# A transformer MLP on one Trainium2 core: the first loads, the transposes of the first x block and its shifted copies rearranged

## The chip, the cores and the metric

The kernel runs on one core of one Trainium2 chip. The metric is device time in microseconds (us) of one execution, as a median of several runs. Beside it stands one profiled execution, whose trace gives the start and the duration of every instruction on TensorE (PE, with its weight loads as PEld), VectorE (DVE), ScalarE (ACT), GpSimd (POOL) and SyncE (SP), and the DMA transfers.

## What is computed

The reference, with B = 1, S = 2048, D = 576, F = 4608, all inputs bfloat16:

```python
h = jnp.einsum("bsd,df->bsf", x, w1) + b1
r = jnp.where(h > zero, h, zero)
h = r * r
out = jnp.einsum("bsf,fd->bsd", h, w2) + b2
```

So two matrix products with a squared ReLU between them. D = 576 is four chunks of 128 and a tail of 64.

## The kernel before, in words

**Blocks.** The 2048 rows of x are cut into four blocks of 512 rows. For each block the first product makes h transposed (F on partitions, 36 tiles of 128), ScalarE adds b1 and applies ReLU (line 176), VectorE squares (line 177). The second product is made in two parts: `phase_t` gives the last 128 output columns transposed, `phase_b` the first 448 columns. The order is blocks 0 and 1 through the first product, then both through the second, then blocks 2 and 3 likewise.

**The first product has two forms.** `a_full` makes 4 of the 36 tiles with four matmuls of 128 rows (chunks k = 0 to 3 of D, weights in `w1n`) and, for the 64-row tail, a `pair` of two matmuls that use the lower and the upper half of the array at the same time (weights in `w1n8`, lines 203 and 205). `a_rows` makes the other 32 tiles wholly in such pairs of 64-row matmuls (lines 188 and 190), 9 pairs for two tiles, with weights in `w1_h`. Its lower and upper halves need every 64-row chunk of x transposed in both partition halves. So the transposed block `xTw` has nine windows of 512 columns, and the shifted windows are made by copies from one partition half to the other (`dup_windows`, lines 119 and 120).

**How x gets transposed.** Blocks 1 to 3 come by transposing DMAs. Block 0 comes as four plain row tiles `x_sb` (j = 0 to 3, 128 rows each) and is transposed on TensorE (`x_transpose`, line 149) into PSUM tiles `tb`, from which `x_copies` (lines 156 to 159) moves them to `xTw`: chunks 0 and 2 and the last 128 columns on VectorE, chunks 1 and 3 on ScalarE. There are five transposes for each row tile: four chunks, and the last 128 columns once more, whose upper half is the 64-column tail.

**The start, in TensorE's order.** Seven matmuls on constants (`WARM`, line 63) fill the time until x is there. Then: ten transposes of row tiles 0 and 1; `part(0, 0)`, which is four matmuls of chunk 0 over the first 256 columns (line 227); five transposes of tile 2; `part(0, 1)` and `part(0, 2)`; five transposes of tile 3; `part(0, 3)`, `part(1, 0)`; one transpose that makes the bias columns `b1T` (lines 166 and 167); `part(1, 1)` to `part(1, 3)`; two pairs; then `a_rows(0)`. All of this order is written out by hand, each engine's instructions stay in program order.

**The loads.** SP's DMA queue has, in order: x tile 0, `w1n` chunks 0 and 1, x tile 3, `w1n` chunks 2 and 3, then `w1_h` in pieces with the two halves of `w1n8` (32 KB each) after the first pair, later x block 1, b2, w2 in four pieces. ACT's queue has x tiles 1 and 2. GpSimd's queue has b1 and a column of b2. Eight DMA semaphores are used in turn on the SP and ACT queues, so an issue waits until the eighth DMA before it has landed.

**PSUM** has eight banks in two pools of four, `ps_h` and `ps_o`. In the first `a_full`, two accumulators lie in each pool, and the transposes use banks of both.

Of the kernel before, what the change touches and what calls it, by code (L numbers as in the profile page):

```python
# [11 lines left out]
BF16 = mybir.dt.bfloat16  # L12
# [5 lines left out]
def kernel(  # L18
# [40 lines left out]
    wps = ps_o.tile([P, 512], FP32, name="wps", tag="po")  # L59
    ones = nc.const_aps.tensor(1.0, [P, 512], BF16)  # L60
    WARM = [512] * 6 + [128]
# [5 lines left out]
    w1n8 = wpool.tile([P, G // 2, P], BF16, name="w1n8")  # L67
# [6 lines left out]
    def load_w1n(eng, k):  # L74
        keep(eng.dma_start(out=w1n[:, k, :], in_=w1[k * P:(k + 1) * P, 0:GW]))

    def load_w1n8(eng, h):
        src = w1[NK * P:D, 0:GW].rearrange("p (i h f) -> p i h f", h=2, f=P)
        keep(eng.dma_start(out=w1n8[h * H:(h + 1) * H, :, :], in_=src[:, :, h, :]))
# [4 lines left out]

    load_x(nc.sync, 0)
    load_x(nc.scalar, 1)
    load_w1n(nc.sync, 0)
    load_x(nc.scalar, 2)
    load_w1n(nc.sync, 1)
    load_x(nc.sync, 3)  # L90
    for k in range(2, NK):
        load_w1n(nc.sync, k)
# [3 lines left out]
    b1_rows = const.tile([P, P], BF16, name="b1_rows")  # L96
    nc.gpsimd.memset(b1_rows[:], 0.0)
    nc.gpsimd.dma_start(out=b1_rows[0:NFT, :], in_=b1.rearrange("(ft p) -> ft p", p=P))
    b2_col = const.tile([P, 1], BF16, name="b2_col")
    nc.gpsimd.dma_start(out=b2_col[:], in_=b2[DM:D].rearrange("(d o) -> d o", o=1))  # L100
    b2T = const.tile([P, 1], FP32, name="b2T")
    nc.gpsimd.tensor_copy(out=b2T[:], in_=b2_col[:])
    warm = const.tile([P, 1], FP32, name="warm")
    keep(nc.scalar.activation(out=warm[:], in_=nc.const_aps.tensor(0.0, [P, 1], FP32), func=ACT.Relu))

# [25 lines left out]
    W2CH = 9  # L131
# [9 lines left out]
    tb_po = [ps_o.tile([P, 2, HS], BF16, name="tb", tag="po") for _ in range(2)]  # L141
    tb_ph = [ps_h.tile([P, 2, HS], BF16, name="tb", tag="ph") for _ in range(4)]
    half_banks = [tb_ph, None]

    def x_transpose(j, k):
        h, q = divmod(j, 2)
        qc = slice(q * P, (q + 1) * P)
        bank, slot, c0 = (half_banks[h][k], 0, k * P) if k < NK else (half_banks[h][2], 1, D - P)
        keep(nc.tensor.transpose(bank[:, slot, qc], xs[:, j, c0:c0 + P], ident[:]))  # L149

    def x_copies(h):
        hc = slice(h * HS, (h + 1) * HS)
        for k in range(NK):
            src = half_banks[h][k][:, 0, :]
            if k % 2 == 0:
                keep(nc.vector.tensor_copy(out=xT0[:, O + k, hc], in_=src))  # L156
            else:
                keep(nc.scalar.copy(out=xT0[:, O + k, hc], in_=src))  # L158
        keep(nc.vector.tensor_copy(out=xT0[:, E3, hc], in_=half_banks[h][2][:, 1, :]))  # L159


    b1T = const.tile([P, NFT], FP32, name="b1T")

    def make_b1T():
        b1T_ps = ps_o.tile([P, P], BF16, name="b1T_ps", tag="po")
        keep(nc.tensor.transpose(b1T_ps[:], b1_rows[:], ident[:]))  # L166
        keep(nc.vector.tensor_copy(out=b1T[:], in_=b1T_ps[:, 0:NFT]))
# [27 lines left out]
    def a_full(sb, order):  # L195
        xT = xT_blk[sb]
        banks = []
        for g in range(G):
            pool, tag = (ps_o, "po") if g < 2 else (ps_h, "ph")
            banks.append(pool.tile([P, SB], FP32, name="pn", tag=tag))  # L200

        def pair(i, start, stop):
            keep(nc.tensor.matmul(banks[2 * i][:], lhsT=w1n8[0:H, i, :], rhs=xT[0:H, SPC, :],  # L203
                             start=start, stop=stop, skip_group_check=order == "k_outer"))
            keep(nc.tensor.matmul(banks[2 * i + 1][:], lhsT=w1n8[H:P, i, :], rhs=xT[H:P, E3, :],  # L205
# [13 lines left out]
        else:  # L219
            if order == "k_outer":  # L220
                tb_new = [ps_h.tile([P, 2, HS], BF16, name="tb", tag="ph") for _ in range(2)]
                half_banks[1] = tb_new + tb_po

# [7 lines left out]
                for j in range(2):  # L231
                    for k in range(NK):
                        x_transpose(j, k)
# [126 lines left out]
```

## Time and profile before

| | |
|---|---|
| median of 4 runs | 291.17 us (290.93 to 291.5) |
| the profiled execution | 291.13 us |
| its span, from the first to the last instruction | 289.4 us |
| first matmul of line 188 (`a_rows(0)` begins) | 10.04 us after the span's start |
| TensorE busy | 285.2 us (99%) |
| VectorE busy | 78.5 us (27%) |
| ScalarE busy | 96.7 us (33%) |

The time of the profiled execution is 1.7 us more than its span. The page gives busy times by engine; the chain of waits follows the last instruction back through what released each step; the timeline gives start and duration of merged groups of instructions, where "x10" means ten instructions and the duration reaches from the first start to the last end. Matmuls overlap: the last one's own duration is part of a group's duration, and the rate is read from starts. All times are counted from the span's start.

### The profile page before, as it was taken

What the parts mean: (1) busy time and instruction counts of PE and PEld (TensorE: products, weight loads), DVE (VectorE), ACT (ScalarE), POOL (GpSimd) and SP (SyncE); (2) the same over time, 40 slices, a digit from 0 to 9 for tenths busy, and PEclk for the clock granted to TensorE, in tenths of its full rate; (3) what the DMA queues carried; (4) which work ended last, traced back from release to release, by engine and by line L of the source; (5) the groups of instructions that cost most, each with busy time, mean ns of one, the idle gap of its engine ahead of it and who ended that gap; (6) DMA issues with size and microseconds to landing.
All of it is one profiled execution on the core that took longest, in us unless ns stands there. A gap on an engine that the chain in (4) does not pass through costs nothing.

```text
span 289.4 us, 4693 instructions
## 1 busy us (share of the span) xinstructions
PE 285.2 (99%) x2027; PEld 139.3 (48%) x2032; DVE 78.5 (27%) x176; ACT 96.7 (33%) x154; POOL 2.3 (1%) x10
## 2 busy tenths in 40 slices
PE   8999999999999999999999999999999999999996
PEld 4544444444444555555544444444444455555555
DVE  1644554444500200000025444444440001100001
ACT  2666666666500000000027667666670000000000
POOL 3000000000000000000000000000000000000000
DMA  6999999400001100000000000000000110000000
GB/s 195 214 242 187 315 388 226 87 0 2 0 18 26 47 16 18 16 16 18 16 16 2 1 2 0 2 0 2 0 2 0 36 39 16 16 16 20 32 16 18
DMA packets 31605, 16.52 MB, mean 57 GB/s; under 512 B 15700, under 2 KB 31584, under 8 KB 31584
## 3 DMA queue, kind: packets, MB, share of 16 engines
q1 hardware_dynamic: 31232, 15.91, 22.1%
q8 instruction: 16, 0.26, 0.4%
q10 hardware_dynamic: 288, 0.30, 0.4%
q14 instruction: 5, 0.04, 0.1%
q0 software_dynamic: 64, 0.01, 0.0%
HBM read 11.36 MB, written 2.36 MB: 47 GB/s over the span
## 4 chain that ended last, share of the span: by engine, by line
PE 97%; DMA 1%; DVE 0%; issue 0%
PE ph L188 42%; PE po L289 38%; PE pt L270 11%; PE pn L209 4%; PE pn L227 1%; DMA x_sb<-in_x_dram 1%; PE tb L149 1%; PE ph L190 1%; PE pn L203 1%; DVE o_sb L291 0%; DVE xTw L156 0%; DVE xTw L159 0%; PE b1T_ps L166 0%; PE pn L205 0%
## 5 line engine op out<-in xcount | busy, mean ns | idle before, releaser
L188 PE MATMUL ph<-xTw,w_h 64*128 64x512 bf16 x576 | 124.6, 376 | 0.0
L190 PE MATMUL ph<-xTw,w_h 64*128 64x512 bf16 x576 | 124.6, 376 | 0.0
L289 PE MATMUL po<-w_sb,hT 128*128 128x448 bf16 (+2 forms) x612 | 109.4, 341 | 0.0
L176 ACT ACTIVATE r<-ph,b1T 128x512 bf16<-128x512 f32 x128 | 81.1, 685 | 41.6 <-PE ph L190 41.6
L188 PEld LDWEIGHTS <-w_h 64*128 64x128 bf16 x576 | 54.1, 94 | 68.3
L289 PEld LDWEIGHTS <-hT 128*128 128x128 bf16 x612 | 58.5, 98 | 51.0
L177 DVE TENSOR_TENSOR hT<-r 128x512 bf16<-128x512 bf16 x144 | 61.2, 426 | 75.9 <-ACT r L176 75.5
L190 PEld LDWEIGHTS <-w_h 64*128 64x128 bf16 x576 | 54.1, 94 | 0.0
L291 DVE TENSOR_TENSOR o_sb<-po,b_bc 128x448 bf16<-128x448 f32 (+2 forms) x17 | 10.2, 597 | 125.8 <-PE po L289 125.8
L270 PE MATMUL pt<-hT,w_sb 128*128 128x512 bf16 x142 | 31.3, 379 | 0.1
L176 ACT ACTIVATE r<-pn,b1T 128x512 bf16<-128x512 f32 x16 | 10.3, 688 | 61.0 <-PE pn L205 59.6
L270 PEld LDWEIGHTS <-w_sb 128*128 128x128 bf16 x144 | 14.1, 98 | 17.0
L273 ACT ACTIVATE oT<-pt,b2T 128x512 bf16<-128x512 f32 x4 | 2.8, 688 | 28.3 <-PE pt L270 28.3
L209 PE MATMUL pn<-xTw,w1n 128*128 128x512 bf16 x45 | 10.4, 379 | 0.4 <-issue 0.3
L209 PEld LDWEIGHTS <-w1n 128*128 128x128 bf16 x48 | 4.5, 98 | 6.0 <-issue 0.8
L227 PE MATMUL pn<-xTw,w1n 128*128 128x256 bf16 x32 | 4.2, 273 | 0.0
L63 PE MATMUL wps<-const-bfloat16-1.0 128*128 128x512 bf16 (+1 forms) x7 | 2.8, 581 | 0.8 <-PEq L344 0.8
L227 PEld LDWEIGHTS <-w1n 128*128 128x128 bf16 x32 | 2.9, 99 | 0.7 <-DMA w1n<-in_w_dram 0.5
L156 DVE COPY xTw<-tb 128x256 bf16<-128x256 bf16 x4 | 1.1, 292 | 6.5 <-PE tb L149 6.5
L119 DVE COPY xTw<-xTw 64x2048 bf16<-64x2048 bf16 x4 | 2.8, 689 | 0.2
L120 DVE COPY xTw<-xTw 64x2048 bf16<-64x2048 bf16 x4 | 2.8, 688 | 0.1
L158 ACT COPY xTw<-tb 128x256 bf16<-128x256 bf16 x4 | 1.3, 375 | 3.5 <-PE tb L149 3.5
(23 smaller groups left out, 15.9 us busy)
## 6 DMA issues: line engine op xcount, KB each, us to landing
w_sb<-in_w_dram SPq DMA_DIRECT2D x4, 1296.0 KB, 11.7
w_h<-in_w_dram SPq DMA_DIRECT2D x14, 288.0 KB, 6.5
out_dram<-o_sb SPq DMA_DIRECT2D x15, 112.0 KB, 1.7
w_h<-in_w_dram SPq DMA_DIRECT2D x4, 144.0 KB, 3.7
w1n<-in_w_dram SPq DMA_DIRECT2D x4, 128.0 KB, 3.9
out_dram<-ot SPq DMA_DIRECT2D x4, 128.0 KB, 2.0
x_sb<-in_x_dram ACTq DMA_DIRECT2D x2, 144.0 KB, 2.9
x_sb<-in_x_dram SPq DMA_DIRECT2D x2, 144.0 KB, 3.4
```

What stands on the lines that cost most here:

```text
L63: keep(nc.tensor.matmul(wps[:, 0:n], lhsT=ones[:, 0:P], rhs=ones[:, 0:n], start=True, stop=True))
L149: keep(nc.tensor.transpose(bank[:, slot, qc], xs[:, j, c0:c0 + P], ident[:]))
L176: keep(nc.scalar.activation(out=r[:], in_=bank[:], func=ACT.Relu, bias=b1T[:, ft:ft + 1], scale=1.0))
L177: keep(nc.vector.tensor_tensor(out=hTs[sb][:, ft, :], in0=r[:], in1=r[:], op=ALU.mult))
L188: keep(nc.tensor.matmul(bx[:], lhsT=w1_h[0:H, LO_C[i], jc], rhs=xT[0:H, LO_W[i], :], start=(i == 0), stop=(i == NC - 1)))
L190: keep(nc.tensor.matmul(by[:], lhsT=w1_h[H:P, UP_C[i], jc], rhs=xT[H:P, UP_W[i], :], start=(i == 0), stop=(i == NC - 1)))
L203: keep(nc.tensor.matmul(banks[2 * i][:], lhsT=w1n8[0:H, i, :], rhs=xT[0:H, SPC, :], start=start, stop=stop, skip_group_check=order == "k_o ...
L209: keep(nc.tensor.matmul(banks[g][:], lhsT=w1n[:, k, g * P:(g + 1) * P], rhs=xT[:, O + k, :], start=start, stop=stop))
L227: keep(nc.tensor.matmul(banks[g][:, hc], lhsT=w1n[:, k, g * P:(g + 1) * P], rhs=xT[:, O + k, hc], start=(h == 0 and k == 0), stop=False, s ...
L270: keep(nc.tensor.matmul(pt[:], lhsT=w2_sb[:, ft, DM:D], rhs=hT[:, ft, :], start=(i == 0), stop=(i == NFT - 1)))
L289: keep(nc.tensor.matmul(po[:, 0:d1 - d0], lhsT=hT[:, ft, jj * P:(jj + 1) * P], rhs=w2_sb[:, ft, d0:d1], start=(i == 0), stop=(i == NFT - 1)))
L291: keep(nc.vector.tensor_tensor(out=o_sb[:, d0:d1], in0=po[:, 0:d1 - d0], in1=b2_bc[:, d0:d1], op=ALU.add))
```

## The change

- **Loads.** ACT's queue has `w1n` chunk 0 first, then x tiles 2 and 3 and `w1n` chunk 3, and after ScalarE's table load b1. SP's queue has x tiles 0 and 1, `w1n` chunks 1 and 2, both halves of `w1n8` (now all 512 columns in each half, 64 KB each), then `w1_h`. GpSimd issues no DMA; the column of b2 goes to SP behind `w1_h`. w2 comes in two pieces in place of four.
- **Transposes.** Four for each row tile, 16 in all. The 64 tail columns of two row tiles are put side by side by GpSimd (`xs8`), and one transpose does both tiles: two transposes in all (`transpose_tails`, into `tl`).
- **Copies out of PSUM.** VectorE takes six of the eight chunk copies, ScalarE the last two. Four copies of 64 partitions move the tails from `tl` to the two windows where the pairs read them.
- **Shifted copies of block 0.** ScalarE makes the lower windows E to E+2 (64 x 1536, `dup_windows_first`); VectorE the upper ones (64 x 2048) and one lower window (64 x 512).
- **Order and banks.** Row tiles 2 and 3 are transposed after `part(0, 0)` and `part(0, 1)`; the bias transpose comes after `part(1, 1)`. All four accumulators of the first `a_full` lie in `ps_o`. The last warm-up matmul has 256 columns in place of 128.

The diff, cut to its core:

```diff
-    WARM = [512] * 6 + [128]
+    WARM = [512] * 6 + [256]
...
-    w1n8 = wpool.tile([P, G // 2, P], BF16, name="w1n8")
+    w1n8 = wpool.tile([P, GW], BF16, name="w1n8")
...
     load_x(nc.sync, 0)
-    load_x(nc.scalar, 1)
-    load_w1n(nc.sync, 0)
+    load_w1n(nc.scalar, 0, 1)
+    load_x(nc.sync, 1)
     load_x(nc.scalar, 2)
-    load_w1n(nc.sync, 1)
-    load_x(nc.sync, 3)
-    for k in range(2, NK):
-        load_w1n(nc.sync, k)
+    load_w1n(nc.sync, 1, 2)
+    load_x(nc.scalar, 3)
+    load_w1n(nc.sync, 2, 3)
+    load_w1n(nc.scalar, 3, 4)
...
-    nc.gpsimd.dma_start(out=b1_rows[0:NFT, :], in_=b1.rearrange("(ft p) -> ft p", p=P))
+    keep(nc.scalar.dma_start(out=b1_rows[0:NFT, :], in_=b1.rearrange("(ft p) -> ft p", p=P)))
+    for h in range(2):
+        load_w1n8(nc.sync, h)
+    xs8 = const.tile([P, RT, H], BF16, name="xs8")
+    for h in range(2):
+        keep(nc.gpsimd.tensor_copy(out=xs8[:, 2 * h:2 * h + 2, :], in_=xs[:, 2 * h:2 * h + 2, NK * P:D]))
...
-    W2CH = 9
+    W2CH = 18
...
+    tb = [[ps_h.tile([P, 4, HS], BF16, name="tb", tag="ph") for _ in range(2)] for _ in range(2)]
+    def x_transpose(j):
         h, q = divmod(j, 2)
+        hc = slice(h * HS, (h + 1) * HS)
+        for bank in range(2):
+            for k in range(2 * bank, 2 * bank + 2):
+                keep(nc.tensor.transpose(tb[h][bank][:, k % 2, q * P:(q + 1) * P], xs[:, j, k * P:(k + 1) * P], ident[:]))
+            for k in range(2 * bank, 2 * bank + 2) if q == 1 else ():
+                copy = nc.scalar.copy if h == 1 and bank == 1 else nc.vector.tensor_copy
+                keep(copy(out=xT0[:, O + k, hc], in_=tb[h][bank][:, k % 2, :]))
...
+    def dup_windows_first():
+        keep(nc.scalar.copy(out=xT0[0:H, E:E + 3, :], in_=xT0[H:P, O:O + 3, :]))
+    def transpose_tails():
+        tl = ps_h.tile([P, 2, P], BF16, name="tl", tag="ph")
+        for h in range(2):
+            keep(nc.tensor.transpose(tl[:, h, :], xs8[:, 2 * h:2 * h + 2, :], ident[:]))
+        x8 = xT0.rearrange("p c (h q t) -> p c h q t", h=2, q=2)
+        for q in range(2):
+            keep(nc.vector.tensor_copy(out=x8[H:P, E3, :, q, :], in_=tl[q * H:(q + 1) * H, 0:2, :]))
+        for q in range(2):
+            keep(nc.vector.tensor_copy(out=x8[0:H, SPC, :, q, :], in_=tl[q * H:(q + 1) * H, 0:2, :]))
+        keep(nc.vector.tensor_copy(out=xT0[H:P, SPC:SPC + 4, :], in_=xT0[0:H, O:O + 4, :]))
+        keep(nc.vector.tensor_copy(out=xT0[0:H, E3, :], in_=xT0[H:P, O + 3, :]))
...
                 for j in range(2):
-                    for k in range(NK):
-                        x_transpose(j, k)
-                for j in range(2):
-                    x_transpose(j, NK)
-                x_copies(0)
-                part(0, 0)
-                for k in range(NK + 1):
-                    x_transpose(2, k)
-                part(0, 1)
+                    x_transpose(j)
+                for k in range(2):
+                    part(0, k)
+                    x_transpose(2 + k)
+                dup_windows_first()
                 part(0, 2)
-                for k in range(NK + 1):
-                    x_transpose(3, k)
-                x_copies(1)
-                dup_windows(0)
+                transpose_tails()
                 part(0, 3)
-                part(1, 0)
-                make_b1T()
-                for k in range(1, NK):
+                for k in range(NK):
                     part(1, k)
+                    if k == 1:
+                        make_b1T()
```

## The prediction

> **What bounds the kernel now.** I read four views in this order: the head of the page, the waits of TensorE behind the start, the chain of waits over the first 11 us, and the timeline of TensorE over the same stretch.
>
> The first part of the page says that TensorE is the bound:
>
> ```profile
> span 289.4 us, 4693 instructions
> PE 285.2 (99%) x2027; PEld 139.3 (48%) x2032; DVE 78.5 (27%) x176; ACT 96.7 (33%) x154; POOL 2.3 (1%) x10
> ```
>
> The waits of TensorE between 10 us and the end hold one line, 0.3 us of issue and no wait for another engine or a DMA. So from the first matmul of line 188, at 10.04 us, to the end the stream is dense, and 289.4 - 10.04 = 279.4 us follow whatever the start looks like. The change touches nothing in TensorE's list behind that point. The question is when `a_rows(0)` begins, and whether its weights come in time. The chain of waits over the start:
>
> ```profile
> 0.74 2.92 DMA x_sb<-in_x_dram
> ...
> 3.70 1.26 PE tb L149 x10
> ...
> 4.98 0.29 DVE xTw L156
> 5.28 0.21 DVE xTw L159
> ...
> 5.53 0.40 PE tb L149 x4
> ...
> 5.96 1.19 PE pn L227 x8
> 7.15 0.28 PE tb L149 x5
> 7.43 0.87 PE pn L227 x8
> ```
>
> The reader is to see that the chain is the landing of x tile 0 (3.65 us), then TensorE, broken once by VectorE's copies at 5 us, then TensorE. The timeline of TensorE gives the rates:
>
> ```profile
> 0.78 2.83 PE L63 MATMUL wps<-const-bfloat16-1.0 128*128 128x512 bf16 x7 [0.78 <-PEq L344]
> 3.70 1.25 PE L149 MATMUL tb<-ident,x_sb 128*128 128x128 bf16 x10
> 4.80 0.60 PE L227 MATMUL pn<-xTw,w1n 128*128 128x256 bf16 x4
> 5.26 0.67 PE L149 MATMUL tb<-ident,x_sb 128*128 128x128 bf16 x5
> 6.99 0.44 PE L149 MATMUL tb<-ident,x_sb 128*128 128x128 bf16 x5
> 8.19 1.47 PE L227 MATMUL pn<-xTw,w1n 128*128 128x256 bf16 x12
> ```
>
> To be seen here: twelve matmuls of 256 columns in 1.47 us, the last of them 0.27 long, give (1.47 - 0.27) / 11 = 0.109 us each. Five transposes in 0.44 us, the last 0.22, give 0.056. But the first ten transposes take 1.25, the last 0.31, so about 0.107: until 4.64 TensorE runs at half rate, and at 4.80 at full rate, although the windows view prints a granted clock of 1.00 throughout. Call this the flip, at about 4.7 us. A pair of 64-row matmuls takes 0.215 (124.6 us / 576 on the page's line of L188).
>
> Check of the old start with these rates: 20 + 1 transposes x 0.056 = 1.18; 32 matmuls x 0.109 = 3.49; two pairs 0.43; about ten transposes at half rate, 0.5 more; together 5.60. From 3.70 to 10.04 are 6.34, so about 0.74 us are gaps. The starts in the trace give them: 0.06 before 4.80, 0.22 before 5.53 (the copy of line 159 frees a PSUM bank), 0.20 before 5.96 and 0.13 before 6.54 (`w1n` chunks 1 and 2 landing), 0.10 before the first pair at 9.60 (nothing waited for; 128-row to 64-row matmuls).
>
> **The change, part by part.**
>
> *Landing times.* By the issues view with windows round single issues, before: x tile 1 (ACT, first) 0.74 + 2.73 = 3.47; tile 0 (SP, first) 3.65; tile 2 (ACT, second) 1.16 + 3.06 = 4.21; chunk 0 (SP, second) 1.20 + 3.18 = 4.38; chunk 1 1.69 + 4.22 = 5.91; tile 3 6.12; chunk 2 6.49; chunk 3 7.07. After, by place in its queue: chunk 0 (ACT, first) about 3.4, tile 0 (SP, first) 3.65, tile 2 (ACT, second) 4.2, tile 1 (SP, second) as the old chunk 0 and 16 KB longer, 4.43. So tile 1 comes 1 us later, and it is now the second thing that TensorE asks for.
>
> *The new start, added up.* Tile 0's four transposes at half rate from 3.70: 0.43, until 4.13. Then TensorE waits for tile 1: 4.43 plus the 0.05 that tile 0 took from landing to its first transpose, 4.48. **This wait of 0.35 is new**; everything on TensorE is queued behind it. VectorE's first copy waits for the second transpose of tile 1 (4.48 + 0.11 = 4.59). In the old rows a transpose at 4.10 released a copy at 4.45 that ended at 4.75 and released the matmul at 4.80: 0.70. With the flip on the way I take 0.65: `part(0, 0)` starts at 5.24, against 4.80. The other transposes of tile 1 are inside that, so **0.44 is lost here**. From there: 32 matmuls x 0.109 = 3.49; 8 + 2 + 1 transposes x 0.056 = 0.62; the 0.10 ahead of the pairs; two pairs 0.43; together 4.64. Before, 10.04 - 4.80 = 5.24 went into the same stretch, as it held as many matmuls and transposes and the three gaps of 0.55 (and 0.05 of odd starts). **0.60 is gained here**, provided that nothing new waits. `a_rows(0)` begins at 5.24 + 4.64 = 9.88, 0.16 earlier.
>
> *Do the waits stay away?* Needed against there, by the same sum: chunk 1 at 5.24 + 0.44 + 0.22 = 5.90; tile 3 at 6.34; chunk 2 at 6.56; chunk 3 at 7.11. Before, the same bytes had landed at 5.91, 6.12, 6.49 and 7.07, but tile 3 stood behind chunk 1. The trace bounds the new times from both sides. While both queues were loaded (2.50 to 3.25) the DMA rate was 363 GB/s: the 272 KB of chunk 1 and tile 3 take 0.75, landing about 5.1. With one queue (4.00 to 4.75) it was 229 GB/s: about 1.2, landing at 5.6, or 6.1 with the last engine as late as for the old tile 3; then chunk 1 costs 0.2, and chunk 2 (landing up to 7.07) up to 0.3 more. I take nothing, as the queue that runs dry in the old rows after 4 us stays loaded now, and keep +0.5 as the end of the range.
>
> A rule bears on those late landings. Chunk 1 took 4.2 us where the issue before it took 3.2, and its last sixteenth came 0.6 after the fifteenth. The Trainium skill, "DMA: Bandwidth & Descriptors", section "Latency and other measured facts", says that two of the sixteen DMA engines are usually slower, and puts it, as a guess, on descriptors of GpSimd's DMAs, of which the change has none. By it the late sixteenth goes and the landings are in time; the sum above already takes that end. Against this, the skill's quick reference ("Trainium Kernel Development and Optimization") says that issuing from several engines saves only issue time, as all run on the same sixteen; by it the slow end holds.
>
> *The copies.* VectorE's row for 128x256 out of PSUM is 0.29, three following each other every 0.22. Tile 3's second transpose starts at 6.40, its copies end by 7.2. The tails' transposes start at 7.00, so the four tail copies run from about 7.3 to 8.3; the trace has no copy of 64 partitions out of PSUM, and I bound it by 0.22 and by the 0.69 of the 64x2048 copy: 8.2 to 10.1. The pairs need them at 9.35. I take 0.25, nearest in elements (256), so 1 us of cover; at the upper end 0.8 would be lost. Then 0.69 (64x2048), about 0.2 (64x512) and 0.2 (b1T), until 9.4; the ninth matmuls of `a_rows` need the first of these only at 10.9, and ScalarE the last at 9.75. ScalarE's own two copies end at 7.4 (0.37, one per 0.27), and the 64x1536 copy at that rate per element takes 6 x 0.27 = 1.6, until 9.1; TensorE needs it at 9.88 + 4 x 0.215 = 10.7. GpSimd's `xs8` copies have no row; its two 128x128 operations take 0.21 and 0.29, tile 3 is there at 5.1 to 6.1, and the tails' transposes need the copies at 7.0, so three times that would still do. I take all of these as hidden.
>
> *SP's queue.* `w1n8` moves ahead of `w1_h`, and the third pieces of `w1_h` are what is tight: issued at 7.71 and 8.40, landing at 12.1 and 13.3, needed two groups of 9 x 0.215 = 1.94 after 10.04, at 13.9. The new order issues the waits in the order chunk 0, tile 0, tile 2, tile 3, chunk 1, chunk 3, chunk 2, each 0.4 to 0.65 of SP; by the landings above the third pieces go out at 7.4 and 8.0. Needed at 13.75. Cover 0.4 to 0.8; nothing lost. Later pieces have 2 us and more. b1 goes out on ACT after tile 1's landing and the table load, at 4.5, and has until 8.4; the old one took 4.0. w2 in two pieces lands by about 47 as before, and is first read at 76.
>
> The last warm-up matmul ends its columns at 3.50, before 3.70: free. Sum: 291.13 - 0.16 = 290.97 on the profiled execution's basis, which lies 0.04 under the median of 291.17; so **291.0** as a median.
>
> **The rivals.**
> 1. *The gain of 0.60 is real and the loss of 0.44 is not* (faster). If tile 1 lands near 3.7, as the old tile 1 did from the other queue, the wait of 0.35 goes, and a flip before 4.1 would take 0.3 off six transposes: together 0.8 under the old start at best, 290.4. Against it: four landings in order, 3.47, 3.65, 4.21, 4.38, which go by bytes.
> 2. *The old waits come back* (within 0.2%). The loads come at the one-queue rate; +0.5 on the sum: 291.5.
> 3. *The flip comes late* (slower). Place: TensorE idles 0.35 and then 0.4 between 4.13 and 5.24, and does transposes alone between 3.55 and 5.24; before, the longest gap there was 0.1. If the flip needs unbroken work, as long as the 3.9 us from 0.78 to 4.7, it comes at 4.48 + 3.9 = 8.4, and the 3.2 us from 5.24 run at half rate: 1.6 lost, 292.5. It decides from a flip at about 6.7 on, where 0.7 is lost. For it: nothing in the trace shows a flip across a gap. Against it: in the trace the flip came within transposes. The Trainium skill ("TensorE: Matmul & The Clock Gate", section "Part 4: PE-mode transpose") says that transposes do not count as busy in the same way, which would speak for this rival; its Part 1 has the gate look at free-running windows of 3.4 us, by which gaps of 0.4 do no harm. No row here tells them apart.
> 4. *Third pieces of `w1_h` or the tail copies late* (slower): 0.8 at the bound above, 291.9.
>
> **How the numbers follow.** A measurement of this kernel can tell about 0.2%, 0.58 us, from no change. Forecast 0.50 (its own range 290.6 to 291.4), rival 2 0.15; both within 0.2%: 0.65. Rival 1 0.13, faster. Rival 3 0.14 and rival 4 0.08, slower: 0.22. The range takes in rival 1's end and rival 4, and leaves out rival 3: 290.4 to 291.9.
>
> **What would show it.** Right: a wait of about 0.35 for the DMA of x tile 1 at 4.1 to 4.5; the first matmul of `part(0, 0)` at 5.2; no waits for `w1n` from there; the first matmul of the rows near 9.9; dense from there. Wrong: matmuls of 256 columns every 0.21 behind 5.3 (rival 3), waits for `w1n` (rival 2), a wait of the pairs for VectorE or of the third group of rows for `w1_h` (rival 4), tile 1 landing under 4 us (rival 1).

## The result, and the profile after

The changed kernel takes 291.26 us in the median (290.93 to 293.27, 46 runs); the kernel before, on the same chip, 291.01 (290.63 to 292.05, 69 runs). The ratio is 1.0012, 95% interval 1.0006 to 1.0018: 0.35 us slower in the mean (0.25 by the medians), where the forecast was 0.16 faster (291.0). The time lies in the range of 290.4 to 291.9 and within 0.2% of the kernel before, but its sign is the other one. Three of the 46 runs lie at 293.0 to 293.3, where the kernel before has none above 292.05; they raise the ratio and leave the median alone.

The profiled execution of the changed kernel took 291.14 us, 0.01 more than that of the kernel before, with a span 0.1 shorter. The head of its page:

```profile
span 289.2 us, 4696 instructions
PE 285.1 (99%) x2025; PEld 159.7 (55%) x2030; DVE 79.3 (27%) x181; ACT 97.5 (34%) x153; POOL 1.5 (1%) x9
```

TensorE is the bound as before. Its chain of waits over the start (start, duration, what):

```profile
1.19 3.15 DMA x_sb<-in_x_dram
4.33 0.05 issue
4.38 0.41 PE tb L149 x2
...
4.81 0.30 DVE xTw L152
...
5.16 0.60 PE pn L231 x4
5.76 0.22 PE tb L149 x4
```

The chain now begins with the landing of x tile 1 (SP's second load, 4.33), not of tile 0. That is the wait that the prediction put at 0.35 us. The timeline of TensorE (start, duration, group) gives the rest of the start:

```profile
3.72 1.26 PE L149 MATMUL tb<-ident,x_sb 128*128 128x128 bf16 x8
5.16 0.60 PE L231 MATMUL pn<-xTw,w1n 128*128 128x256 bf16 x4 [0.17 <-DVE xTw L152]
...
7.07 1.47 PE L231 MATMUL pn<-xTw,w1n 128*128 128x256 bf16 x12
...
9.85 0.38 PE L195 MATMUL ph<-xTw,w_h 64*128 64x512 bf16 x1
```

`part(0, 0)` begins at 5.16 (summed: 5.24; before: 4.80), no gap over 0.1 follows, and `a_rows(0)` begins at 9.85 (summed: 9.88; before: 10.04). In this execution the start went as it was added up, and 0.19 us came in. Part of it went again in the third group of rows. The waits of TensorE's weight loads between 9 and 72 us:

```profile
PEld L197 <- DMA w_h<-in_w_dram: 0.2, 1, 0.2
```

The upper third piece of `w1_h` is issued at 8.84 (summed: 8.0) and lands at 13.81; the group that needs it begins 0.13 late. The end of the span is 0.07 shorter than before (last matmul to the end: 2.65 against 2.72). Net, the span is 0.13 shorter.

**What lies outside the span** is the rest of the difference: time minus span was 1.78 us in the profiled execution of before and 1.92 in this one. Over the timed runs its mean is 1.79 to 1.83 for the kernel before and 1.92 to 1.96 for the changed one, from one group of runs to the next.

### The profile page after: what moved, and what is told of

Same layout as the page of the kernel before. It is cut to its first block, busy times and chain, and to the rows that moved or that the text cites. A ratio compares the mean times of both kernels' runs of the same rounds, so it can differ in the third digit from the quotient of the medians.

```text
span 289.2 us, 4696 instructions
## 1 busy us (share of the span) xinstructions
PE 285.1 (99%) x2025; PEld 159.7 (55%) x2030; DVE 79.3 (27%) x181; ACT 97.5 (34%) x153; POOL 1.5 (1%) x9
## 4 chain that ended last, share of the span: by engine, by line
PE 97%; DMA 1%; issue 0%; DVE 0%; SPq 0%
PE po L286 38%; PE ph L195 30%; PE ph L197 13%; PE pt L267 11%; PE pn L216 4%; PE pn L231 1%; DMA x_sb<-in_x_dram 1%; PE pn L210 1%; PE tb L149 0%; SPq L72 0%; DVE xTw L152 0%; DVE o_sb L288 0%; PE pn L212 0%; PE tl L162 0%; PE b1T_ps L173 0%
## 5 line engine op out<-in xcount | busy, mean ns | idle before, releaser
L288 DVE TENSOR_TENSOR o_sb<-po,b_bc 128x448 bf16<-128x448 f32 (+2 forms) x17 | 10.2, 597 | 125.8 <-PE po L286 125.8
L210 PE MATMUL pn<-xTw,w1n 64*128 64x512 bf16 x8 | 2.4, 379 | 0.0
L212 PE MATMUL pn<-xTw,w1n 64*128 64x512 bf16 x8 | 2.4, 379 | 0.0
```

The source lines that it names most:

```text
L210: keep(nc.tensor.matmul(banks[2 * i][:], lhsT=w1n8[0:H, 2 * i * P:(2 * i + 1) * P], rhs=xT[0:H, SPC, :], start=start, stop=stop, skip_grou ...
L288: keep(nc.vector.tensor_tensor(out=o_sb[:, d0:d1], in0=po[:, 0:d1 - d0], in1=b2_bc[:, d0:d1], op=ALU.add))
```

## The experiments

Each kernel was timed in five rounds against the kernel before on the same chip (11 or 12 runs). Beside the ratio, two numbers were taken of each run: its span, and time minus span ("outside"). "Control" is the kernel before, run beside it. "List" is the number of instructions that the trace records on ScalarE, with its DMA issues and waits.

| kernel | list | outside, us | mean span minus control, us | ratio (95%) |
|---|---|---|---|---|
| e2 | 307 | 1.84 | +0.02 | 1.0003 (0.9995 to 1.0012) |
| e3 | 308 | 1.82 | +0.55 | 1.0022 (1.0008 to 1.0037) |
| e5 | 307 | 1.83 | -0.16 | 0.9996 (0.9988 to 1.0005) |
| e8 | 307 | 1.81 | +0.08 | 1.0002 (0.9991 to 1.0012) |
| e12 | 307 | 1.81 | +0.11 | 1.0002 (0.9988 to 1.0015) |
| e16 | 308 | 1.83 | -0.21 | 0.9999 (0.9990 to 1.0009) |
| e10 | 309 | 1.79 | -0.17 | 0.9992 (0.9980 to 1.0003) |
| e13 | 309 | 1.79 | -0.37 | 0.9990 (0.9981 to 0.9998) |
| e15 | 309 | 1.83 | -0.16 | 0.9995 (0.9985 to 1.0006) |
| e19 | 309 | 1.82 | -0.27 | 0.9988 (0.9979 to 0.9998) |
| e4 | 310 | 1.96 | +0.25 | 1.0017 (1.0003 to 1.0032) |
| e7 (changed kernel again) | 310 | 1.96 | +0.06 | 1.0010 (1.0001 to 1.0019) |
| e18 (changed kernel again) | 310 | 1.92 | +0.35 | 1.0013 (0.9997 to 1.0029) |
| e9 | 310 | 1.94 | +0.15 | 1.0013 (1.0001 to 1.0024) |
| e14 | 310 | 1.95 | -0.20 | 1.0000 (0.9990 to 1.0009) |
| e1 | 312 | 1.95 | +0.04 | 1.0004 (0.9995 to 1.0013) |
| e6 | 312 | 1.94 | -0.06 | 1.0005 (0.9996 to 1.0013) |
| e17 (before again) | 306 | 1.79 | +0.06 | 1.0002 (0.9993 to 1.0011) |

### First: one part of the change undone or done alone

e1: `w1n8` issued by ScalarE, so that SP reaches the third pieces of `w1_h` earlier. e2: the kernel before, without DMAs of GpSimd. e3: the changed kernel with the two small loads on GpSimd's queue again.

```diff
# e1, against the changed kernel
-        load_w1n8(nc.sync, h)
+        load_w1n8(nc.scalar, h)
# e2, against the kernel before; e3 is the same edit backwards in the changed kernel
-    nc.gpsimd.dma_start(out=b1_rows[0:NFT, :], in_=b1.rearrange("(ft p) -> ft p", p=P))
...
-    nc.gpsimd.dma_start(out=b2_col[:], in_=b2[DM:D].rearrange("(d o) -> d o", o=1))
...
+    keep(nc.scalar.dma_start(out=b1_rows[0:NFT, :], in_=b1.rearrange("(ft p) -> ft p", p=P)))
...
+    keep(nc.sync.dma_start(out=b2_col[:], in_=b2[DM:D].rearrange("(d o) -> d o", o=1)))
```

> The changed kernel, but the two loads of w1n8 are issued by ScalarE behind b1, no longer by SP ahead of w1_h. In the changed kernel SP issued the third pieces of w1_h at 8.16 and 8.84 and TensorE stood 0.13 us at the third group of rows, as the upper piece landed at 13.8. Theory (the start was gained as summed and part of it is lost at the third group, as SP's list got longer): the upper third piece is issued at about 8.2, lands by 13.2, the stall is gone, and the time is 0.1 to 0.2 us under the changed kernel. Rival (that stall is a by-product of the transfers' total rate, or chance of the one profile): the landing stays at 13.6 or later and the time stays within 0.1 us of the changed kernel.

> The kernel before, with one part of the change alone: b1 is loaded on ScalarE's queue behind the table load and the column of b2 on SP's queue ahead of the broadcast of b2; GpSimd issues no DMA. In the two profiles the time lies 1.78 us above the span before and 1.92 after, so 0.14 us were added outside the span. Theory (the part outside the span comes from GpSimd's DMAs being gone): time less span goes to about 1.92, the span ends 0.07 us earlier (one wait less on SP at the end), and no landing of w1n is as late as 5.9; time within 0.1 us of before. Rival (the part outside the span has another source): time less span stays at 1.78 and the time falls by 0.07 or more.

> The changed kernel, but with b1 and the column of b2 loaded by GpSimd's queue as before; ScalarE's queue has no b1. Theory (outside the span): time less span goes back from 1.92 to about 1.78 and the time is 0.05 to 0.15 us under the changed kernel, if the landings of w1n do not get later. Rival: time less span stays 1.92 and the time is the same or higher.

e1: the upper third piece is issued at 7.87 and lands at 12.96. Of the waits of weight loads between 9 and 16 us only this line is left, and none for `w_h`:

```profile
PEld L210 <- issue: 0.2, 1, 0.2
```

So the wait of 0.13 is SP's queue, and goes; but the mean span stays where the changed kernel's is (+0.04 here, +0.06 in e7), so it was not the bulk of the loss. e2: chunk 1 lands at 4.84 in place of 5.91, the waits for `w1n` are gone and the rows begin at 9.57 in the profile; yet the mean span does not move (+0.02). Outside the span it has 1.84, where its theory said 1.92; e3 has 1.82, near the 1.78 that its theory said. e3 is the one kernel clearly slower inside the span: chunk 1 lands at 6.00, two waits of 0.24 and 0.26 for `w1n`, rows at 10.31. Its median span is 289.7 against 289.4 of the control (the mean holds one run of 293.6). The changed kernel did not run beside it; as its median span lay 0.2 over (e7) and 0.1 under (e18) its controls, GpSimd's DMAs cost some 0.1 to 0.4 us with this order of the loads.

### Second: gaps filled, the old order of the loads, a longer list

e4 puts constant matmuls where TensorE idles for tile 1 and for the first copy. e5 is the changed kernel with the kernel before's order of the loads. e6 is the kernel before with six more small activations on ScalarE, into a tile that nothing reads; e7 is the changed kernel again.

```diff
# e4, against the changed kernel
-                for j in range(2):
+                for j, fill in ((0, (256,)), (1, (256, 128))):
                     x_transpose(j)
+                    for n in fill:
+                        keep(nc.tensor.matmul(banks[3][:, 0:n], lhsT=ones[:, 0:P], rhs=ones[:, 0:n], start=True, stop=True,
+                                              skip_group_check=True))
# e5, against the changed kernel
-    load_w1n(nc.scalar, 0, 1)
-    load_x(nc.sync, 1)
+    load_x(nc.scalar, 1)
+    load_w1n(nc.sync, 0, 1)
...
-    load_x(nc.scalar, 3)
+    load_x(nc.sync, 3)
...
-    load_w1n(nc.scalar, 3, 4)
+    load_w1n(nc.sync, 3, 4)
# e6, against the kernel before
-    keep(nc.scalar.activation(out=warm[:], in_=nc.const_aps.tensor(0.0, [P, 1], FP32), func=ACT.Relu))
+    for _ in range(7):
+      keep(nc.scalar.activation(out=warm[:], in_=nc.const_aps.tensor(0.0, [P, 1], FP32), func=ACT.Relu))
```

> The changed kernel with three matmuls on constants more (256 columns behind row tile 0's transposes, 256 and 128 behind tile 1's), so that TensorE works through the two gaps of 0.36 and 0.48 us ahead of part(0, 0). They are in the shadow of the wait for x tile 1 and of VectorE's first copy. Theory (the idle gaps make TensorE's full rate come later in many executions, and one window later, 2 us, in a few: 3 of 46 runs of the changed kernel lay at 293.0 to 293.3): no run above 292.3, and the mean span falls by 0.1 to 0.3 us against the changed kernel on the same chip. Rival (the flip to full rate does not depend on such gaps): mean span within 0.1 us, the rare 293 us runs stay.

> The changed kernel with the x and w1n loads in the order and on the queues of before (x tile 1 first on ScalarE's queue, w1n chunk 0 second on SP's); w1n8 stays ahead of w1_h on SP. Theory (the wait for x tile 1 is 0.35 us of the start, and behind it nothing waits): part(0, 0) starts at 4.8 in place of 5.16 and the rows begin at 9.5, unless w1n chunks 1 and 2 land after 5.5 and 6.15; the third group of rows waits for w1_h by up to 0.4; time 0.1 to 0.3 us under the changed kernel. Rival (loads as a whole bind, the order only moves the wait): waits for w1n come back, 0.3 us and more, the rows begin at 9.8 or later, time as the changed kernel.

> The kernel before with six more 128x1 activations on ScalarE behind its table load (0.2 us each, over by 4.5 us, ScalarE's first copy may slip 0.1). ScalarE's list in the profile has 306 instructions before, 307 without GpSimd DMAs, 308 in the changed kernel with them, 310 in the changed kernel; time less span is 1.79, 1.84, 1.82 and 1.95. Theory (what is outside the span grows with ScalarE's list): time less span 1.95. Rival (it does not): 1.79.

> The changed kernel itself, unaltered, on the same chip as the three others: a control, and a second profile of it. If the first profile is typical, the rows begin at 9.8 to 9.9, the third group waits 0.1 for w1_h, and time less span is 1.95. If the loads and the flip to full rate vary, the rows begin up to 0.4 us later.

e4 has one run of 293.4 of its own although the gaps are filled, and its mean span did not fall, so idle time ahead of `part(0, 0)` is not shown to be what makes the runs near 293. Its profile has a wait that the changed kernel's lacks, though no GpSimd DMA is there (waits of TensorE's matmuls between 3.4 and 10 us):

```profile
PE pn L231 <- DMA w1n<-in_w_dram: 0.5, 1, 0.5
```

Chunk 1 landed at 6.47 there, its last sixteenth 1.09 after the fifteenth. e5 is 0.4 us faster than e7 on the same chip: 0.13 outside the span, 0.23 inside. e6 has the loads, waits and copies of the kernel before and only a longer list: 1.94 outside against 1.80 of its control. That started the theory that the length of ScalarE's list makes the difference outside the span.

### Third: the loads by themselves

e8 takes two of the four loads off ScalarE's queue but leaves tile 1 second on SP's. e9 has the new order of the loads in the kernel before (without GpSimd's DMAs). e10 is e5 with `w1n8` on ScalarE; e12 is e5 with `w1n8` loaded as in the kernel before, after the first pair of `w1_h`.

```diff
# e8, against the changed kernel
-    load_x(nc.scalar, 3)
+    load_x(nc.sync, 3)
-    load_w1n(nc.scalar, 3, 4)
+    load_w1n(nc.sync, 3, 4)
# e9, against e2
-    load_x(nc.scalar, 1)
-    load_w1n(nc.sync, 0)
+    load_w1n(nc.scalar, 0)
+    load_x(nc.sync, 1)
...
-    load_x(nc.sync, 3)
-    for k in range(2, NK):
-        load_w1n(nc.sync, k)
+    load_x(nc.scalar, 3)
+    load_w1n(nc.sync, 2)
+    load_w1n(nc.scalar, 3)
# e10, against e5
-        load_w1n8(nc.sync, h)
+        load_w1n8(nc.scalar, h)
# e12, against e5 (its tile and matmul operands as in the kernel before)
-    for h in range(2):
-        load_w1n8(nc.sync, h)
...
+        if j0 == 0:
+            load_w1n8(nc.sync, 0)
+            load_w1n8(nc.sync, 1)
```

> The changed kernel, but x tile 3 and w1n chunk 3 are issued by SP again (SP: x0, x1, w1n 1, x3, w1n 2, w1n 3; ScalarE: w1n 0, x2, b1); w1n 0 stays first on ScalarE's queue and x tile 1 second on SP's, so the wait for tile 1 stays. ScalarE's list goes from 310 to 308. Theory (four loads on ScalarE's queue make the chunks land late, and the list of 310 costs 0.13 us outside the span): time minus span 1.82 instead of 1.95; w1n 1 lands by 5.0, w1n 3 by 6.5 (6.79 in the changed kernel); the row groups begin at 9.85 or before; the span is 0.1 to 0.2 shorter than the changed kernel's; median 0.2 to 0.3 below it, about 291.0. Rival (the wait for tile 1 is what costs): the span is as the changed kernel's, 289.3 to 289.4, and only the 0.13 outside it goes.

> The kernel before, with b1 on ScalarE's queue instead of GpSimd's (as in e2) and with the changed kernel's order of the loads: w1n 0 first on ScalarE, x tile 1 second on SP, then x2, w1n 1 SP, x3 ScalarE, w1n 2 SP, w1n 3 ScalarE. Transposes, copies, w1n 8 and the shifted copies stay as before: the loads' half of the change alone. Theory: against e2 (291.08, mean span 289.31, outside 1.84) the span grows by 0.2 to 0.3 (tile 1 later, chunks later) and the part outside by 0.1 where the list passes 308: median 291.3 to 291.5. Rival (the load order costs nothing by itself; the loss comes from the new transposes and copies): 291.0 to 291.1, as e2.

> The kernel of e5 (changed kernel with the old load order), with the two loads of w1n 8 issued by ScalarE behind b1 instead of by SP; ScalarE's list 310. Theory: no wait for the third group's w_h (0.2 in e5), so the span is 0.1 to 0.2 shorter than e5's 289.11, about 288.95; outside 1.95 instead of 1.82; median 290.9, as e5. Rival (the list isn't the cause of the time outside the span): outside stays at 1.82 and the median is 290.75.

> The kernel of e5 with w1n 8 loaded as in the kernel before (32 KB halves, issued after the first pair of w1_h, not ahead of it); ScalarE's list 308. Theory: SP reaches the third pieces of w1_h earlier than in e5 (8.70), the third group doesn't wait for w_h (0.2 in e5), w1n 8 still lands before it is needed at 9.4; span 0.1 shorter than e5's 289.11, outside 1.82, median 290.8. Rival (the third group's wait was not on the path in most runs): 290.9, as e5. A miss would be a wait of the row group's pairs for w1n 8 after 9.4.

e8: outside 1.81 as expected, and chunk 1 earlier (5.16), but the mean span is the changed kernel's: the rival was right there. In its profile the rows begin at 9.68, but the third group waits for `w1_h`, as two loads more stand ahead of the pieces on SP; from the first matmul of the rows to the last of all it takes 276.97 us, where the kernel before takes 276.59, so 0.38 is given back there (waits of weight loads, 3.4 to 16 us):

```profile
PEld L197 <- DMA w_h<-in_w_dram: 0.5, 1, 0.5
```

e9 has the expected sign (+0.15 in the mean span against e2's +0.02), but the intervals of the ratios overlap. e10 seemed to speak against the list, as 1.79 came where 1.95 was expected; but its trace records 309 instructions on ScalarE and not the 310 of the expectation (e5's 307 and the two issues). e12 missed: SP issued the upper third piece no earlier than in e5 (8.79 against 8.70), it landed at 13.45, and as the rows had begun at 9.37 the third group waited for it all the same (waits of weight loads, 9 to 16 us):

```profile
PEld L196 <- DMA w_h<-in_w_dram: 0.4, 1, 0.4
```

From the first matmul of the rows to the last of all it takes 276.83 us, 0.24 more than the kernel before; the mean span is 0.11 over the control.

### Fourth: where the list steps, and the loads once more

e13 and e14 are the kernel before with three and four more activations (as e6). e15 and e16 make one copy of ScalarE's last two out of PSUM, in the changed kernel and in e10.

```diff
# e15, against the changed kernel; e16, against e10
+            if q == 1 and h == 1 and bank == 1:
+                keep(nc.scalar.copy(out=xT0[:, O + 2:O + 4, hc], in_=tb[h][bank][:, 0:2, :]))
+                continue
             for k in range(2 * bank, 2 * bank + 2) if q == 1 else ():
-                copy = nc.scalar.copy if h == 1 and bank == 1 else nc.vector.tensor_copy
-                keep(copy(out=xT0[:, O + k, hc], in_=tb[h][bank][:, k % 2, :]))
+                keep(nc.vector.tensor_copy(out=xT0[:, O + k, hc], in_=tb[h][bank][:, k % 2, :]))
```

> The kernel before with three further 128x1 activations on ScalarE at its start, into a tile that nothing reads: 309 instructions on ScalarE in the trace instead of 306. Theory (the time outside the span steps up when the list grows from 309 to 310; in the runs so far 306 to 309 gave 1.79 to 1.84 us and 310 to 312 gave 1.94 to 1.96): 1.80, median as the kernel before. Rival (it grows evenly with the list, 0.025 us each): 1.87. Rival (it has to do with ScalarE's DMA issues and the six activations of e6 were chance): 1.79.

> The kernel before with four further 128x1 activations on ScalarE: 310 instructions, one more than in the run with 309. Theory (a step between 309 and 310): 1.94 outside the span, 0.14 more than with 309, median about 0.15 above the kernel before. Rival (even growth): 1.89, 0.025 more than with 309. Rival (DMA issues): 1.79.

> The changed kernel with the two ScalarE copies of tile 3 (L152, columns of w1n chunks 2 and 3) made one copy of both: ScalarE's list 309 instead of 310, all loads as in the changed kernel. Theory (step between 309 and 310): 1.80 outside the span instead of 1.95; span as the changed kernel's, 289.35 in the mean; median 291.1. Rival (what lies outside the span comes from the five DMA issues on ScalarE's queue): 1.95, median 291.26.

> The kernel of e10 (old load order, w1n 8 on ScalarE's queue) with the same two copies made one: ScalarE's list 308. The transposes and copies of the change without its load order and without its longer list, and the candidate to beat both kernels. Theory (the load order costs 0.15 to 0.2 in the span, the list 0.15 outside): against the run with the changed kernel's load order in this call the span is 0.15 to 0.25 shorter (289.1), outside 1.80 in both; median 290.8 to 290.9, 0.1 to 0.2 under the kernel before. Rival (the load order costs nothing in the span): the spans of the two agree within 0.1 and the median is as the kernel before.

The heads of the pages of e13, then of e14:

```profile
span 288.7 us, 4701 instructions
PE 285.2 (99%) x2032; PEld 139.4 (48%) x2032; DVE 78.5 (27%) x176; ACT 97.3 (34%) x157; POOL 2.3 (1%) x10
```

```profile
span 289.2 us, 4702 instructions
PE 285.7 (99%) x2032; PEld 139.6 (48%) x2032; DVE 78.5 (27%) x176; ACT 97.5 (34%) x158; POOL 2.3 (1%) x10
```

They differ by one instruction, the 158th of ACT (310 with its DMA issues, waits and branches). Outside the span that one instruction is worth 0.16 us: 1.79 against 1.95. Taking one away from the changed kernel (e15) brings it back to 1.83. This is shown, in both directions and without any change of the loads. The rivals, an even growth or the DMA issues on ScalarE's queue, fall: e10 issues five DMAs there as the changed kernel does, and has 1.79.

e15 and e16 differ in the order of the loads and in the queue of `w1n8`, and their lists, 309 and 308, lie on the same side of the step; their spans agree within 0.05 us. By this pair the new order of the loads costs nothing, by e5 and e7 it cost 0.23. By the scatter of 12 spans on each side the standard error of such a difference is about 0.13, so what it costs is not settled.

### Fifth: how far two identical kernels lie apart

e17 is the kernel before beside itself, e18 the changed kernel for a third time.

> The kernel before, unchanged, as a kernel of its own beside its own control: how far two identical kernels stand apart, and a second profile of it. Theory (the waits of 0.60 us before the row groups in the first profile of it come and go with the landings: w1n chunk 1 landed at 5.91 there, at 4.88 in the kernel with three activations more, which had no such wait and began its rows at 9.44): rows begin at 9.4 to 9.7 if chunk 1 lands before 5.2, at 9.7 to 10.1 if it lands after 5.4; span within 0.2 of the control's mean in the mean. Rival (0.60 of waits are there in every execution): rows at 10.0 wherever chunk 1 lands.

> The changed kernel, unchanged, once more on the chip of e17: a third profile and twelve more times. Theory (outside the span +0.15 from ScalarE's list; inside it no difference in the mean, because the waits that the change removes are there in a part of the executions only, and the changed kernel, dense from the first chunk on, pays half of every microsecond by which TensorE's full rate comes later): 1.95 outside, span within 0.2 of the kernel before's on this chip, median 0.1 to 0.3 above. Rows begin at 9.37 to 10.2: 9.4 + half of what the full rate is later than 4.5, plus any wait for a chunk. Rival (the start is 0.16 earlier in every execution): span 0.2 shorter than the kernel before's.

e17's mean span lies 0.06 above that of its own control. With e6, e13 and e14 there are four kernels that do the work of the kernel before, and their mean spans lie from 0.37 under to 0.06 over their controls: a difference of 0.2 between two kernels is not shown by 12 runs of each. The profile of e17 shows the waits that the change removes, larger than in the first profile (TensorE's timeline):

```profile
5.79 0.61 PE L227 MATMUL pn<-xTw,w1n 128*128 128x256 bf16 x4
6.79 0.61 PE L227 MATMUL pn<-xTw,w1n 128*128 128x256 bf16 x4 [0.40 <-DMA w1n<-in_w_dram]
...
10.29 0.38 PE L188 MATMUL ph<-xTw,w_h 64*128 64x512 bf16 x1
```

In e13, whose loads are the same (its line numbers are one higher), chunk 1 landed at 4.88 in place of 5.74, and the parts follow each other without a wait:

```profile
5.51 1.04 PE L228 MATMUL pn<-xTw,w1n 128*128 128x256 bf16 x8
...
9.44 0.38 PE L189 MATMUL ph<-xTw,w_h 64*128 64x512 bf16 x1
```

So the same work begins its rows at 10.29 in one execution and at 9.44 in another. e18 shows the second thing that moves them, TensorE's rate:

```profile
5.07 1.01 PE L231 MATMUL pn<-xTw,w1n 128*128 128x256 bf16 x4 [0.17 <-DVE xTw L152]
5.88 0.63 PE L149 MATMUL tb<-ident,x_sb 128*128 128x128 bf16 x4
6.30 0.83 PE L231 MATMUL pn<-xTw,w1n 128*128 128x256 bf16 x4
...
10.52 0.38 PE L195 MATMUL ph<-xTw,w_h 64*128 64x512 bf16 x1
```

Four matmuls in 1.01 in place of 0.60: half rate until 6.5, where it was full from 5.16 in the first profile. There is no wait behind 5.07, and the rows begin 0.67 later, over the 10.2 that was expected as the latest. Of the runs of e18 two lie near 293 (292.9 and 293.2); its median span is 0.1 below its control's.

### Last: the idle time filled in the fastest kernel

```diff
# e19, against e10
                 for j in range(2):
                     x_transpose(j)
+                for n in (256, 128):
+                    keep(nc.tensor.matmul(banks[3][:, 0:n], lhsT=ones[:, 0:P], rhs=ones[:, 0:n], start=True, stop=True,
+                                          skip_group_check=True))
```

> The kernel of e10 (transposes and copies of the change, old load order, w1n 8 on ScalarE's queue, list 309), with two constant matmuls (256 and 128 columns, into a bank that part(0,0) then begins anew) in the 0.37 us in which TensorE waits for the first DVE copy. In the profiles so far TensorE's full rate came at 3.3 to 5.6 (mean 4.3 of 7) with the old transposes, which leave TensorE no such idle time, and at 3.3 to 6.5 (mean 5.2 of 12) with the new ones, and each microsecond of it moves the row groups by half. Theory (the idle time ahead of part(0,0) is why the full rate comes later): the full rate comes by 4.7 in this profile and the mean span is 0.2 to 0.4 shorter than e10's distance to its control (-0.17), so 0.4 to 0.5 under the control here; median 290.6, which would beat both kernels. Rival (when the full rate comes is chance, and has nothing to do with this gap): span 0.1 to 0.2 under the control, as e10, median 290.85, and the full rate anywhere from 3.3 to 6.5.

```profile
4.35 0.52 PE L238 MATMUL pn<-const-bfloat16-1.0 128*128 128x256 bf16 x2
4.72 1.01 PE L231 MATMUL pn<-xTw,w1n 128*128 128x256 bf16 x4
...
10.03 0.38 PE L195 MATMUL ph<-xTw,w_h 64*128 64x512 bf16 x1
```

290.6 us in the median, ratio 0.9988 (0.9979 to 0.9998): the only one of the kernels with the change's transposes whose interval lies under 1. It was not run beside the changed kernel; the two ratios, 0.9988 and 1.0012, are about 0.7 us apart. But e13 lies as far under 1 (0.9981 to 0.9998) with the work of the kernel before, so that e19 is faster is not shown. And the profile speaks against the reason: with the gap filled (4.35 to 4.72) TensorE is at half rate until 6.1 all the same, and the span, 0.27 under the control, lies between what the two theories gave.

## Why the prediction was wrong

**The sum of the start was right for the execution that it was made for.** Wait for tile 1: summed 0.35 with a landing at 4.43; it landed at 4.33 and the wait was 0.26. `part(0, 0)`: 5.24, measured 5.16. From there dense: 4.64, measured 4.69. Rows: 9.88, measured 9.85. The copies were hidden as said (the four tail copies took 0.29 to 0.30 each and ended at 8.47, ScalarE's 64x1536 copy ended at 8.82).

**The step that failed** is the last one, "291.13 - 0.16 = 290.97 on the profiled execution's basis". It failed in two ways.

1. *It took what lies outside the span as fixed.* The table of before named it (1.7 us more than the span) and the sum carried it over, so that what the change adds there was put at nothing without a reason. It is not fixed: the change lengthens ScalarE's list from 306 to 310, and the step of 0.15 us lies between 309 and 310 (e13 against e14, and e15 against the changed kernel). This alone turns -0.16 into about nothing, and it is the part of the loss that is shown. Nothing in one trace would have told it; time minus span of two kernels does.

2. *It took one execution's waits and one execution's flip as the kernel's.* "0.60 is gained here" is read from the rows of one execution, in which chunk 1 landed at 5.91, and "with the flip on the way" takes it at 4.7. Over the profiles of this study both move by more than the gain. Last matmul at half rate: 3.3 to 5.6 us in seven profiles with the old transposes, 3.3 to 6.5 in thirteen with the new ones. Two kernels that differ in `w1n8` and one copy, both without a wait between the begin of `part(0, 0)` and the rows, show what that does (e12, then e16):

```profile
4.73 0.60 PE L230 MATMUL pn<-xTw,w1n 128*128 128x256 bf16 x4 [0.17 <-DVE xTw L151]
...
9.37 0.38 PE L194 MATMUL ph<-xTw,w_h 64*128 64x512 bf16 x1
```

```profile
4.73 1.01 PE L233 MATMUL pn<-xTw,w1n 128*128 128x256 bf16 x4 [0.17 <-DVE xTw L154]
...
10.11 0.38 PE L197 MATMUL ph<-xTw,w_h 64*128 64x512 bf16 x1
```

Same begin, 4.73; the flip at 4.3 in one and at 6.2 in the other; rows 0.74 apart. A start without gaps pays about half of each microsecond by which the flip comes later. The old start has waits for data in which a late flip costs less: e14, flip at 5.6, rows at 9.91; the first profile of before, flip at 4.64, rows at 10.04 (chunk 1 landed at 5.47 and 5.91, so this pair is no proof). In the five profiles with the work and the loads of before (before, e6, e13, e14, e17) the rows begin at 9.44 to 10.29, in the mean 9.88; in the three of the changed kernel at 9.85, 9.95 and 10.52, in the mean 10.11: no earlier, as far as so few profiles tell. So the gain inside the span, -0.13 between the two first profiles, is not the gain of the kernels: in e7 and e18 the mean span is 0.06 and 0.35 over the control, the median 0.2 over and 0.1 under it. The ratio of 1.0012, 0.35 us, is then made up of 0.15 outside the span, which is shown, some 0.12 of the three runs near 293 (3 of 46, each about 1.8 above the rest), whose cause is open, and a rest of less than 0.1 inside it, where -0.13 to -0.16 was to come; that landings and flips account for this last part is argued from single profiles.

**The two queues.** "I take nothing, as the queue that runs dry ... stays loaded now" was wrong in what it assumes. Chunk 1 is issued by SP at 1.65 to 1.69 in every kernel; its landing, without GpSimd DMAs: 4.67 to 5.18 in the six profiles with the old order, two x tiles and b1 first on ScalarE's queue (e2, e5, e10, e12, e16, e19), 5.47 to 6.47 in the six of the new transposes with four loads and b1 there (the changed kernel's three, e1, e4, e15). So with more on ScalarE's queue it came later, with one exception: e9, which has the new order with the old transposes, at 4.97. In the changed kernel's first profile chunk 1 and tile 3 landed at 5.55 and 6.13, at the slow end of the prediction's bounds (5.6 to 6.1) and not at 5.1. It cost nothing in that profile, since `part(0, 1)` begins only at 5.82; in e4 it cost 0.5.

The late last sixteenth of chunk 1 did not go altogether with GpSimd's DMAs: 0.53 behind the fifteenth in the changed kernel's first profile, 1.09 in e4. But it became rare: it is more than 0.4 behind in four of the six profiles with GpSimd's DMAs and in these two of the fourteen without, of which the other twelve have at most 0.24. The Trainium skill's guess of its cause ("DMA: Bandwidth & Descriptors", "Latency and other measured facts") agrees with most of these rows and does not cover the two. The landing itself goes the same way with the old order: 4.88 to 5.91 in the five profiles with GpSimd's DMAs, 4.67 to 5.18 in the six without. The rule of its quick reference ("Trainium Kernel Development and Optimization"), by which a second issuing engine saves issue time only, stood nearer to the runs than the sum did.

**SP's queue.** Third pieces summed at 7.4 and 8.0, issued at 8.16 and 8.84, as SP waits for the landing of x tile 3 (6.13) before an issue. "Cover 0.4 to 0.8; nothing lost" was 0.13 lost (rival 4, in small), in two of the three profiles of the changed kernel. It costs more the earlier the rows begin, as 0.38 in e8 and 0.24 in e12 show. The upper piece landed at 13.81, 13.92 and 13.51 in the three profiles; two groups of 1.94 before that is 9.9, 10.0 and 9.6, so by this estimate rows that begin earlier give the difference back. In the five profiles with the work and the loads of before it landed at 13.01 to 13.38.

**The rivals.** 1 did not come: tile 1 landed at 4.25 to 4.33 in the three profiles. 2 came in e3 and e4, not in the changed kernel's own profiles. 3, in the form of a flip at 8.4, did not come in any profile; but the flip does come at 6.5 (e18), and costs 0.67 there. In e6, e13, e14 and e17 the flip falls among transposes, so transposes did not hold it off. Whether the new start makes it later (mean 5.3 of thirteen against 4.3 of seven) or that is chance stays open: e19 filled the gap and its profile still has it at 6. The skill's page "TensorE: Matmul & The Clock Gate", Part 1, has the gate look at free-running windows of 3.4 us; flips spread over 3.3 to 6.5 with the same warm-up from 0.77 on agree with that, and are wider than the 0.5 us to either side that the page gives for it.

**Open.** Why the runs near 293 are there: 5 of 69 runs of the changed kernel and 2 of 60 of the five kernels with its order of the loads under other edits (e1, e3, e4, e9, e15), none of some 350 runs of the kernel before and of those with the old order. Why e13's span is 0.37 under its control, when its work is the control's. What the order of the loads costs in the mean: between 0 and 0.25 us.

## What to carry to other kernels

An expected gain of 0.2 us out of 290 is under what one profile can show: compare the landings and the rate of two or three profiles of the same kernel before a wait in it is counted as won. Count time minus span as a term of its own, and look at it in every run: here one instruction added to ScalarE's list cost about 0.15 us there, with nothing to see inside the span. A start that has been made dense has no slack left to hide a late clock or a late load; a wait removed there is worth what it was in the mean, not what it was in one trace.

## What the runs showed of the hardware

- The time outside the span steps by 0.15 us between 309 and 310 instructions on ScalarE: 1.79 to 1.84 in the eleven rows of the table with 306 to 309, 1.92 to 1.96 in the seven with 310 to 312. What makes the step was not tried, nor whether other engines' lists have one.
- TensorE went to full rate anywhere between 3.3 and 6.5 us after the span's start, from one profile to the next (20 profiles, warm-up from 0.77 or 0.78 on; half rate is 0.107 us for 128 columns, full rate 0.056), while the profile prints a granted clock of 1.00 throughout.
- The landing of a load whose issue does not move went with how the first loads are spread over the two queues: 4.7 to 5.2 us (six profiles, two x tiles first on ScalarE's) or 5.5 to 6.5 (six, four loads there) for the same 128 KB issued at 1.65 to 1.69, all without GpSimd's DMAs; one profile with four loads there (e9) has 5.0.
